# Scores of two tiles at once in every second step, a new order of the steps, and later first loads of values and words, in a chunked-attention, soft-MoE and SoLU kernel

## The chip, the cores and the metric

The kernel runs on one core of a Trainium2 chip. The metric is device time in microseconds (us), the median of several executions. Engines are called PE or TensorE (matrix products and transposes), DVE or VectorE, ACT or ScalarE, POOL or GpSimd, and SP, which issues the loads from HBM; the 16 DMA engines move the data.

## The reference, cut to what matters

```python
# attention inside chunks of 64 rows; q, k, v are (8, 8, 576, 64)
scores = scale * np.matmul(q_c, k_c.transpose(0, 1, 2, 4, 3))
scores = scores - np.max(scores, axis=-1, keepdims=True)
attn = np.exp(scores); attn = attn / (np.sum(attn, axis=-1, keepdims=True) + 1e-09)
x = np.matmul(attn, v_c)                     # then reshaped to (4608, 512)
# soft mixture of experts: 8 experts, 4 slots each
logits = x @ phi                             # (4608, 32)
d = softmax(logits, axis=0);  slot_input = d.T @ x
for e in range(E):
    h = np.maximum(slot_input[e] @ w1[e], 0.0);  slot_out[e] = h @ w2[e]
x = softmax(logits, axis=1) @ slot_out
# SoLU layer
h = x @ w_in;  solu = h * softmax(h)
ln = (solu - mean) / sqrt(var + 1e-06) * g_ln;  out = ln @ w_out
```

## The kernel before, in words

The 4608 rows are 36 tiles of 128. The first stage goes over the tiles in steps 0 to 33 (the last two tiles are in a list behind it). Each step works on several tiles at once, one behind the other: `S` makes the scores of tile i on PE (8 matmuls per tile), `mx` and `sub` take the row maximum and subtract it on DVE, `exp` is on ACT; `PT` transposes the result of tile i-1 and `PTe` copies it out of PSUM on ACT; `x` multiplies tile i-2 with the values, `rz`, `rc` and `xm` divide by the sums; `xT` transposes tile i-3, `xTe` copies it, and once in four steps `LT`, `L`, `mT`, `sl`, `z` and their helpers keep a running softmax over the rows. Beside it every step from 2 on converts one chunk c of the 64-bit words in which the SoLU weights are given: `t` (line 210) and `sq` (206) on ACT, `u` (213) and `a` (223) on DVE, `m` (219), `add` (229) and `mul` (233) on POOL. `m` needs the `sq` of its chunk, and the `sq` of the next chunk writes the buffer that `mul` reads, so one conversion follows the other in a ring over ACT and POOL.

The order of the operations of a step is written by hand: `STEP` has one line for each of the four kinds of steps (i modulo 4), and every engine gets its instructions in that order. Loads are issued by SP in the same order: `qk` loads the queries and keys of tile i+4 (two loads of 256 KB, into one of four buffers), `v` the values of two tiles, `raw` the words of two chunks, `W` the expert weights as far as the table `PACE` lets them. `FIRST` lists the loads ahead of step 0. The loads use eight semaphores in turn (DMAHW0 to DMAHW7), and a load waits until the load eight places before it has landed.

In the kernel before, the scores of even and odd tiles are the two halves of one PSUM tile `sx` (line 249). Behind the steps a list `ORDER` goes on: the last two tiles, the experts (lines 936, 973 and 987 multiply with `w1`, `w2` and the last columns of `w2`, as their weights come in), the combination with the slots, and from some 193 us on the SoLU output tiles, whose products are line 1393.

Of the kernel before, what the change touches and what calls it, by code (L numbers as in the profile page):

```python
# [9 lines left out]
F32 = mybir.dt.float32  # L10
# [7 lines left out]
PSUM = bass.MemoryType.PSUM  # L18
# [8 lines left out]


STEP = """
S a m t x xT u mT qk rz PT mx v xTe sub PTe W rc add mul raw exp xm mn d sq de  # L30
S a x u raw v m qk rz sl mx t W rc z xT sub xTe PT PTe add xm acc mul sq exp
m t S u a x qk rz xT mx W sub xTe PT rc acc v PTe add LT xm mul sq raw exp lte
t m a S x u raw L tm v mx xT add qk PT lall rz mul xTe sub rc PTe W sq xm exp
"""
PACE = [
    0, 0, 0, 0, 0, 0, 0, 1, 2, 2, 3, 4, 4, 5, 6, 6, 7, 8, 8, 9, 10, 10, 11, 12, 13, 13, 14, 15,
# [4 lines left out]
""".split()  # L41
AHEAD = 8
GATE = dict()
FIRST = "cs qk0 qk1 qk2 v0 raw0 qk3 g phi v2 raw2 raw4"
ORDER = """
cq1 cq2 cq3 cq4 cq5 cq6 cq7 S34 S35 loadw xT31 mx34 mx35 PT33 x32 xtev31 rz32 ptev33 sub34 LT31 lte7 ev32 own_c exp34
x33 own_q PT34 ptev34 xT32 L7 rz33 sub351 sub350 x34 exp350 PT350 exp351 ev33 xtev32 ptev0 xT33 PT351 lall7 LT32 rz34
# [20 lines left out]
def soft_moe_kernel(ctx: ExitStack, tc, qkT, v1, w12, w64, phi, g_ln, cst, out):  # L68
# [10 lines left out]
    cs = const.tile([128, 257], F32, name="cs")  # L79
# [18 lines left out]
    acc = mp.tile([128, 512], F32, name="acc")  # L98
# [136 lines left out]
    def cv_c(c):  # L235
# [1 line left out]

    first_loads = dict(
        qk0=lambda: load_qk(0), qk1=lambda: load_qk(1), qk2=lambda: load_qk(2), qk3=lambda: load_qk(3), v0=lambda: load_v(0), v2=lambda: load_v(2),
        **{f"raw{i}": lambda i=i: load_raw(i) for i in range(6)},  # L240
        cs=lambda: nc.sync.dma_start(out=cs, in_=cst), phi=lambda: nc.sync.dma_start(out=phi_sb, in_=phi),
        g=lambda: nc.sync.dma_start(out=g_sb, in_=g_ln),
    )
# [2 lines left out]

    p_t, pt_t, xps_t, x_t, lt_t, sps_t, mx_t = {}, {}, {}, {}, {}, {}, {}

    sx = ps1.tile([128, 2, 512], F32, name="s_ps")

    def pe_S(i):
        s = sx[:, i % 2, :]
        b = qk[i % 4]
        for g in range(4):
            for c in range(2):
                nc.tensor.matmul(  # L256
                    s[ts(c, 64), ts(g, 128)], b[:, 1, ts(2 * g + c, 64)], b[:, 0:3:2, ts(2 * g + c, 64)],
                    start=True, stop=True, tile_position=(0, 64 * c),
                )
        sps_t[i] = s.rearrange("p (h k) -> p h k", k=64)  # L260
# [210 lines left out]
    def step_ops(i):  # L471
        s0, s1, s2, s3, s4 = (blk(n, i) for n in (6, 7, 8, 9, 10))
        if i == NT - 3:
            s4 = s3
        c = cstep.get(i, NRAW)
        st = {}

        def rz():
            st["xp"] = x_view(xps_t[i - 2])
            st["rz"] = x_sums(st["xp"])  # L480

        def rc():
            mark("rc", nc.vector.reciprocal(out=st["rz"], in_=st["rz"]))

        def xm():
            x_t[i - 2] = x = XB[(i - 2) % 7]
            mark("xm", nc.vector.tensor_tensor(
                out=heads(x), in0=st["xp"][:, :, :, 0:64],
                in1=st["rz"].to_broadcast([128, 2, 4, 64]), op=ALU.mult,
            ))  # L490

        def W():
            load_w(pace[i + 1] - pace[i])

        cvc, x2, x3 = c < NRAW, i >= 2, i >= 3
        return dict(
            u=(cvc, lambda: cv_u(c)), m=(cvc, lambda: cv_m(c)), a=(cvc, lambda: cv_a(c)), add=(cvc, lambda: cv_s(c)),
            mul=(cvc, lambda: cv_w(c)), raw=(cvc, lambda: load_raw(c + 5)),
            sq=(True, lambda: cv_sq(cstep.get(i + 1, NRAW))), t=(True, lambda: cv_t(cstep.get(i + 1, NRAW))),
            S=(True, lambda: pe_S(i)), qk=(True, lambda: load_qk(i + 4)),  # L500
            mx=(True, lambda: soft_max(i)), sub=(True, lambda: soft_sub(i)), exp=(True, lambda: exp_S(i)),
            PT=(i >= 1, lambda: PTm(i - 1)), PTe=(i >= 1, lambda: PTe(i - 1)),
            x=(x2, lambda: pe_x(i - 2)), v=(i >= 1, lambda: load_v(i + 3)),
            rz=(x2, rz), rc=(x2, rc), xm=(x2, xm),
            xT=(x3, lambda: xTm(i - 3)), xTe=(x3, lambda: xTe(i - 3)), LT=(x3, lambda: pe_LT(i - 3)),
            lte=(s0 is not None, lambda: blk_a(s0)),
            L=(s1 is not None, lambda: pe_L(s1)), lall=(s1 is not None, lambda: blk_l(s1)),
            tm=(s1 is not None, lambda: run_max(s1)),
            mT=(s2 is not None, lambda: mTm(s2)), mn=(s2 is not None, lambda: mnv(s2)),
            d=(s2 is not None, lambda: dv(s2)),  # L510
            de=(s2 is not None, lambda: de(s2)),
            z=(s3 is not None, lambda: zm(s3)), sl=(s3 is not None, lambda: slm(s3)),
            acc=(s4 is not None, lambda: blk_e2(s4)), W=(True, W),
        )
# [63 lines left out]


    def x34():  # L580
        xps_t[n - 1] = x = sx
        pt = pt_t.pop(n - 1)
        for g in range(4):
            x_mm(n - 1, x, pt[:, g, :], g)
# [285 lines left out]

    def open_2():
        nonlocal e1, ps2, soT, cz, mx
        p1.close()
        e1 = pool("e1", 1)
        ps2 = pool("ps2", 1, p2, space=PSUM)
        T["hTb"] = e1.tile([128, 512], F32, name="hTb")
        soT = e1.tile([128, 4, 32], F32, name="soT")
        T["cP"] = e1.tile([128, 2, 128], F32, name="cP")
        cz = e1.tile([128, NT], F32, name="cz")
        mx = e1.tile([128, 9], F32, name="wmx")  # L880
# [617 lines left out]
```

## Time and profile before

| | us |
|---|---|
| three executions | 403.80, 402.84, 403.44 (median 403.44) |
| the profiled execution | 402.77 |
| its span in the trace | 401.0 |
| PE busy | 382.4 (95%) |
| DVE busy | 311.0 (78%) |
| ACT busy | 224.3 (56%) |
| POOL busy | 200.2 (50%) |

The span is the time from the first to the last instruction in the trace, and 1.77 us of the profiled execution lie outside it. The busy shares are means over all stages. The 16 DMA engines are busy all the time until about 181 us and only partly afterwards, so the first 181 us and the rest have to be read apart.

### The profile page before, as it was taken

What the parts mean: (1) busy time and instruction counts of PE and PEld (TensorE: products, weight loads), DVE (VectorE), ACT (ScalarE), POOL (GpSimd) and SP (SyncE); (2) the same over time, 40 slices, a digit from 0 to 9 for tenths busy, and PEclk for the clock granted to TensorE, in tenths of its full rate; (3) what the DMA queues carried; (4) which work ended last, traced back from release to release, by engine and by line L of the source; (5) the groups of instructions that cost most, each with busy time, mean ns of one, the idle gap of its engine ahead of it and who ended that gap; (6) DMA issues with size and microseconds to landing.
All of it is one profiled execution on the core that took longest, in us unless ns stands there. A gap on an engine that the chain in (4) does not pass through costs nothing. (4 is left out here: it accounts for less than half of the span.)

```text
span 401.0 us, 10317 instructions
## 1 busy us (share of the span) xinstructions
PE 382.4 (95%) x3947; PEld 220.4 (55%) x3947; DVE 311.0 (78%) x777; ACT 224.3 (56%) x470; POOL 200.2 (50%) x201
## 2 busy tenths in 40 slices
PE   3799899999999999999999999999999999999997
PEld 2577777777787642354544444444444444444445
DVE  3788788989886449574989799999888888888840
ACT  1577877877785512332577765556554555455521
POOL 2577767777778246330123255555455544454430
PEclk9999999999999999999999999999999999999999
DMA  7999999999999999991156757777665666557671
GB/s 231 403 409 408 389 397 397 409 407 407 410 397 408 401 396 406 409 391 26 30 103 146 140 134 159 159 158 148 144 140 135 144 151 133 132 137 158 132 159 52
DMA packets 101153, 99.20 MB, mean 247 GB/s; under 512 B 78064, under 2 KB 78704, under 8 KB 101104
## 3 DMA queue, kind: packets, MB, share of 16 engines
q1 hardware_dynamic: 101104, 98.54, 77.1%
q8 instruction: 31, 0.51, 0.5%
q14 instruction: 18, 0.15, 0.1%
HBM read 70.60 MB, written 9.44 MB: 200 GB/s over the span
## 5 line engine op out<-in xcount | busy, mean ns | idle before, releaser
L1194 POOL TENSOR_SCALAR uh<-u,sc 128x1024 f16<-128x1024 f32 (+1 forms) x35 | 65.1, 1860 | 51.1 <-issue 38.3
L1393 PEld LDWEIGHTS <-uhT 128*128 128x128 f16 x560 | 52.1, 98 | 68.3 <-issue 8.8
L1393 PE MATMUL o_ps<-xb,uhT 128*128 128x512 f16 x280 | 66.7, 380 | 0.7 <-DMA uhT<-uh 0.7
L1393 PE MATMUL o_ps<-xb,ulT 128*128 128x512 f16 x280 | 66.3, 379 | 0.0
L1393 PE MATMUL o_ps<-wo,uhT 128*128 128x512 f16 x280 | 66.1, 379 | 0.0
L1322 ACT ACTIVATE e<-h_ps,nm 128x1024 f32<-128x1024 f32 x34 | 37.8, 1113 | 43.7 <-DVE nm L1316 43.7
L1210 ACT ACTIVATE e<-u,nmean 128x1024 f32<-128x1024 f32 x35 | 40.1, 1147 | 28.7 <-DVE nmean L1209 28.7
L256 PE MATMUL s_ps<-qk 128*64 128x128 f32 x576 | 41.1, 287 | 9.3 <-DMA qk<-in_qkT 6.5
L1360 POOL TENSOR_TENSOR a<-a,mhalf 128x1 f32<-128x1 f32 x36 | 21.8, 606 | 56.2 <-DVE a L1377 42.5
L1316 DVE TENSOR_REDUCE nm<-h_ps 128x1 f32<-128x1024 f32 x34 | 41.5, 1220 | 9.3 <-PE h_ps L1311 9.3
L1185 DVE SCALAR_TENSOR_TENSOR u<-h_ps,e 128x1024 f32<-128x1024 f32 x35 | 42.8, 1223 | 6.1 <-ACT e L1322 6.1
L1393 PEld LDWEIGHTS <-ulT 128*128 128x128 f16 x280 | 27.3, 98 | 33.1 <-issue 0.3
L1370 DVE SCALAR_TENSOR_TENSOR ul<-u,sc,uh 128x1024 f16<-128x1024 f32 x35 | 45.3, 1295 | 0.0
L256 PEld LDWEIGHTS s_ps<-qk 128*64 128x64 f32 x576 | 32.5, 141 | 16.2 <-issue 10.3
L398 ACT ACTIVATE xt_b<-xt_ps 128x512 f32<-128x512 f32 (+1 forms) x37 | 21.6, 586 | 17.8 <-PE xt_ps L416 16.9
L265 DVE TENSOR_REDUCE mx<-s_ps 128x8 f32<-128x512 f32 x36 | 24.6, 684 | 8.5 <-PE s_ps L256 8.0
L1411 ACT ACTIVATE ob<-o_ps,a 128x512 f32<-128x512 f32 x35 | 23.8, 679 | 9.3 <-PE o_ps L1393 8.0
L219 POOL TENSOR_SCALAR conv<-conv 128x256 f32<-128x256 f32 x16 | 17.6, 1099 | 21.8 <-ACT conv L206 21.8
L1311 PE MATMUL h_ps<-s,c4T 128*128 128x512 f32 x68 | 27.4, 485 | 0.0
L277 ACT ACTIVATE p<-p 128x512 f32<-128x512 f32 x35 | 21.7, 621 | 6.6 <-DVE p L271 6.6
L271 DVE TENSOR_TENSOR p<-s_ps,mx 128x512 f32<-128x512 f32 x35 | 24.1, 690 | 0.9
L229 POOL TENSOR_TENSOR conv<-conv 128x256 int32<-128x256 int32 x32 | 23.3, 729 | 2.6
(232 smaller groups left out, 633.5 us busy)
## 6 DMA issues: line engine op xcount, KB each, us to landing
w<-in_w SPq DMA_DIRECT2D x45, 512.0 KB, 8.0
qk<-in_qkT SPq DMA_DIRECT2D x72, 256.0 KB, 6.8
vall<-in_v SPq DMA_DIRECT2D x18, 520.0 KB, 6.7
out<-ob SPq DMA_DIRECT2D x35, 256.0 KB, 2.1
raw<-in_w SPq DMA_DIRECT2D x16, 512.0 KB, 6.4
qk<-in_w SPq DMA_DIRECT2D x4, 512.0 KB, 9.0
w_raw<-in_w SPq DMA_DIRECT2D x3, 512.0 KB, 9.0
vall<-in_w SPq DMA_DIRECT2D x3, 512.0 KB, 8.9
```

Source lines behind the costliest of these rows:

```text
L256: nc.tensor.matmul(s[ts(c, 64), ts(g, 128)], b[:, 1, ts(2 * g + c, 64)], b[:, 0:3:2, ts(2 * g + c, 64)], start=True, stop=True, tile_posit ...
L265: mark("mx", nc.vector.tensor_reduce(out=mx, in_=s, axis=AX.X, op=ALU.max))
L271: mark("sub", nc.vector.tensor_tensor(out=p, in0=s, in1=mx.unsqueeze(2).to_broadcast([128, 8, 64]), op=ALU.subtract,))
L1185: nc.vector.scalar_tensor_tensor(out=u, in0=d["h"], scalar=1.0, in1=e, op0=ALU.mult, op1=ALU.mult, accum_out=zz[:, 1:2])
L1194: nc.gpsimd.tensor_scalar(out=uh[:, 0:n], in0=u[:, 0:n], scalar1=d["sc"][:, 1:2], scalar2=1.0, op0=ALU.mult, op1=ALU.mult)
L1210: nc.scalar.activation(out=d["e"], in_=d["u"], func=AF.Square, bias=nmean, scale=1.0, accum_out=d["zz"][:, 2:3])
L1311: nc.tensor.matmul(h[:, ts(n, 512)], c4T[:, i, :], s4[n], start=True, stop=True)
L1316: nc.vector.tensor_reduce(out=nm, in_=st[i]["h"], axis=AX.X, op=ALU.max, negate=True)
L1322: nc.scalar.activation(out=d["e"], in_=d["h"], func=AF.Exp, bias=d["nm"], scale=1.0, accum_out=d["zz"][:, 0:1])
L1370: nc.vector.scalar_tensor_tensor(out=ul, in0=d["u"], scalar=d["sc"][:, 1:2], in1=d["uh"], op0=ALU.mult, op1=ALU.subtract)
L1393: nc.tensor.matmul(d["o"], lt(n % 8), w(n % 8), start=(n == 0), stop=(n == 23))
L1411: nc.scalar.activation(out=ob, in_=d["o"], func=AF.Copy, scale=d["a"][:, 7:8])
```

## The change

The diff is short and stands here with one of the four lines of `STEP`. `pe_S` writes two separate PSUM tiles, `s0` and `s1`. In even steps it is called for tile i and tile i+1, one behind the other, and in odd steps not at all. The four lines of `STEP` are in a new order. In `FIRST` the loads `v2`, `raw2` and `raw4` are left out and `g` and `phi` go ahead of `qk3`; `v2` and `raw2` follow behind the q and k of tile 4 (step 0), `raw4` behind those of tile 5 (step 1). The two PSUM tiles are given back before the product of tile 34 and a tile of their old joint size takes their place.

```diff
--- before.py
+++ after.py
@@ -27,10 +27,10 @@
 
 
 STEP = """
-S a m t x xT u mT qk rz PT mx v xTe sub PTe W rc add mul raw exp xm mn d sq de
...
+S x t v m a rz xT u qk xTe PT mT PTe mx W sub add rc exp mul xm mn sq d raw de
...
 """
 PACE = [
     0, 0, 0, 0, 0, 0, 0, 1, 2, 2, 3, 4, 4, 5, 6, 6, 7, 8, 8, 9, 10, 10, 11, 12, 13, 13, 14, 15,
@@ -41,7 +41,8 @@
 """.split()
 AHEAD = 8
 GATE = dict()
-FIRST = "cs qk0 qk1 qk2 v0 raw0 qk3 g phi v2 raw2 raw4"
+FIRST = "cs qk0 qk1 qk2 v0 raw0 g phi qk3"
+THEN = {0: 'v2 raw2', 1: 'raw4'}
 ORDER = """
 cq1 cq2 cq3 cq4 cq5 cq6 cq7 S34 S35 loadw xT31 mx34 mx35 PT33 x32 xtev31 rz32 ptev33 sub34 LT31 lte7 ev32 own_c exp34
 x33 own_q PT34 ptev34 xT32 L7 rz33 sub351 sub350 x34 exp350 PT350 exp351 ev33 xtev32 ptev0 xT33 PT351 lall7 LT32 rz34
@@ -237,7 +238,7 @@
 
     first_loads = dict(
         qk0=lambda: load_qk(0), qk1=lambda: load_qk(1), qk2=lambda: load_qk(2), qk3=lambda: load_qk(3), v0=lambda: load_v(0), v2=lambda: load_v(2),
-        **{f"raw{i}": lambda i=i: load_raw(i) for i in range(6)},
+        **{f"raw{i}": lambda i=i: load_raw(i) for i in range(6)}, v4=lambda: load_v(4), v6=lambda: load_v(6),
         cs=lambda: nc.sync.dma_start(out=cs, in_=cst), phi=lambda: nc.sync.dma_start(out=phi_sb, in_=phi),
         g=lambda: nc.sync.dma_start(out=g_sb, in_=g_ln),
     )
@@ -246,10 +247,13 @@
 
     p_t, pt_t, xps_t, x_t, lt_t, sps_t, mx_t = {}, {}, {}, {}, {}, {}, {}
 
-    sx = ps1.tile([128, 2, 512], F32, name="s_ps")
+    pss = ctx.enter_context(ExitStack())
+    ps_s = pool("ps_s", 1, pss, space=PSUM)
+    s_banks = [ps_s.tile([128, 512], F32, name="s_ps", tag=f"s{a}") for a in range(2)]
+    sx = None
 
     def pe_S(i):
-        s = sx[:, i % 2, :]
+        s = s_banks[i % 2]
         b = qk[i % 4]
         for g in range(4):
             for c in range(2):
@@ -479,6 +483,11 @@
             st["xp"] = x_view(xps_t[i - 2])
             st["rz"] = x_sums(st["xp"])
 
+        def q():
+            load_qk(i + 4)
+            for o in THEN.get(i, "").split():
+                first_loads[o]()
+
         def rc():
             mark("rc", nc.vector.reciprocal(out=st["rz"], in_=st["rz"]))
 
@@ -497,7 +506,7 @@
             u=(cvc, lambda: cv_u(c)), m=(cvc, lambda: cv_m(c)), a=(cvc, lambda: cv_a(c)), add=(cvc, lambda: cv_s(c)),
             mul=(cvc, lambda: cv_w(c)), raw=(cvc, lambda: load_raw(c + 5)),
             sq=(True, lambda: cv_sq(cstep.get(i + 1, NRAW))), t=(True, lambda: cv_t(cstep.get(i + 1, NRAW))),
-            S=(True, lambda: pe_S(i)), qk=(True, lambda: load_qk(i + 4)),
+            S=(i % 2 == 0, lambda: (pe_S(i), pe_S(i + 1))), qk=(True, q),
             mx=(True, lambda: soft_max(i)), sub=(True, lambda: soft_sub(i)), exp=(True, lambda: exp_S(i)),
             PT=(i >= 1, lambda: PTm(i - 1)), PTe=(i >= 1, lambda: PTe(i - 1)),
             x=(x2, lambda: pe_x(i - 2)), v=(i >= 1, lambda: load_v(i + 3)),
@@ -578,6 +587,9 @@
 
 
     def x34():
+        nonlocal sx
+        pss.close()
+        sx = pool("ps_sx", 1, pss, space=PSUM).tile([128, 2, 512], F32, name="s_ps")
         xps_t[n - 1] = x = sx
         pt = pt_t.pop(n - 1)
         for g in range(4):
@@ -870,6 +882,7 @@
 
     def open_2():
         nonlocal e1, ps2, soT, cz, mx
+        pss.close()
         p1.close()
         e1 = pool("e1", 1)
         ps2 = pool("ps2", 1, p2, space=PSUM)
```

The first place is SP at the start, from the first words (`raw`, line 189 before and 190 after) on. Before, the words of chunks 2 to 5 are the last two rows but two:

```order
L189 DMA raw<-in_w 128x1024 [waits DMAHW0_49]
L176 DMA qk_114<-in_qkT 64x1024 [waits DMAHW1_49,DVE_49]
L176 DMA qk_114<-in_qkT 64x1024 [waits DMAHW2_49,Pool_49]
L242 DMA g_sb<-in_g_ln 128x8 [waits DMAHW3_49]
L241 DMA phi_sb<-in_phi 128x128 [waits DMAHW4_49]
L181 DMA vall<-in_v 128x1040 [waits DMAHW5_49]
L189 DMA raw<-in_w 128x1024 [waits DMAHW6_49]
L189 DMA raw<-in_w 128x1024 [waits DMAHW7_49]
L176 DMA qk_111<-in_qkT 64x1024 [waits DMAHW0_49,PE_49]
L176 DMA qk_111<-in_qkT 64x1024 [waits DMAHW1_49]
```

After, they are one by one behind the q and k of tiles 4 and 5 (buffers qk_111 and qk_112 for the second time):

```order
L190 DMA raw<-in_w 128x1024 [waits DMAHW0_49]
L243 DMA g_sb<-in_g_ln 128x8 [waits DMAHW1_49]
L242 DMA phi_sb<-in_phi 128x128 [waits DMAHW2_49]
L177 DMA qk_114<-in_qkT 64x1024 [waits DMAHW3_49,DVE_49]
L177 DMA qk_114<-in_qkT 64x1024 [waits DMAHW4_49,Pool_49]
L177 DMA qk_111<-in_qkT 64x1024 [waits DMAHW5_49,PE_49]
L177 DMA qk_111<-in_qkT 64x1024 [waits DMAHW6_49]
L182 DMA vall<-in_v 128x1040 [waits DMAHW7_49]
L190 DMA raw<-in_w 128x1024 [waits DMAHW0_49]
L177 DMA qk_112<-in_qkT 64x1024 [waits DMAHW1_49,PE_49]
L177 DMA qk_112<-in_qkT 64x1024 [waits DMAHW2_49]
L190 DMA raw<-in_w 128x1024 [waits DMAHW3_49]
```

The load of the second words (`raw`) moves from two places behind `phi` and the values to behind four halves of q and k; it now waits for DMAHW0, which is the first words' own semaphore, where before it waited for DMAHW6, a half of q and k.

The second place is PE in steps 8 and 9, in the middle of the first stage. Before:

```order
L256 MATMUL s_ps<-qk_111 64x128 [waits DMAHW4_49,DMAHW3_49,DVE_49]
L256 MATMUL s_ps<-qk_111 64x128 x7
L282 MATMUL x_ps<-vall,pt 64x65 [waits DMAHW0_49,DVE_49,Activation_49]
L282 MATMUL x_ps<-vall,pt 64x65 x15
L416 MATMUL xt_ps<-cs,xb_85 128x128 [waits PE_49]
L416 MATMUL xt_ps<-cs,xb_85 128x128 x3
L423 MATMUL mT_ps<-cs,ltb 128x128
L407 MATMUL pt_ps<-cs,p 128x128 [waits PE_49,Activation_49]
L407 MATMUL pt_ps<-cs,p 128x128 x3
L256 MATMUL s_ps<-qk_112 64x128 [waits DMAHW7_49,DMAHW0_49,DVE_49]
L256 MATMUL s_ps<-qk_112 64x128 x7
L282 MATMUL x_ps<-vall,pt 64x65 [waits DVE_49,Activation_49]
```

After:

```order
L260 MATMUL s_ps<-qk_111 64x128 [waits DMAHW4_49,DMAHW3_49]
L260 MATMUL s_ps<-qk_111 64x128 x7
L260 MATMUL s_ps<-qk_112 64x128 [waits DMAHW6_49,DMAHW5_49,DVE_49]
L260 MATMUL s_ps<-qk_112 64x128 x7
L286 MATMUL x_ps<-vall,pt 64x65 [waits DMAHW1_49,DVE_49,Activation_49]
L286 MATMUL x_ps<-vall,pt 64x65 x15
L420 MATMUL xt_ps<-cs,xb_85 128x128 [waits PE_49]
L420 MATMUL xt_ps<-cs,xb_85 128x128 x3
L411 MATMUL pt_ps<-cs,p 128x128 [waits Activation_49]
L411 MATMUL pt_ps<-cs,p 128x128 x3
L427 MATMUL mT_ps<-cs,ltb 128x128
```

The scores of step 9 have moved into step 8, ahead of that step's product with the values (`x_ps`), and the first of the two score groups has no wait for DVE any more; the second keeps one.

## Rows read from the trace of the kernel before

**Rows 1.** the page's first line
```profile
span 401.0 us, 10317 instructions
```

**Rows 2.** the chain of work that ended last: start us, us, what
```profile
206.86 5.35 PE o_ps L1393 x24
```

**Rows 3.** windows: busy us (instructions) per engine, then clock, DMA share, GB/s
```profile
15.00:20.00 5.00, 3.54 (x69) 2.85 (x70) 3.74 (x8) 2.96 (x7) 4.12 (x5) 1.00 1.03 414
40.00:45.00 5.00, 4.66 (x108) 3.74 (x108) 3.43 (x8) 4.33 (x11) 3.15 (x5) 1.00 0.99 385
45.00:50.00 5.00, 4.29 (x97) 3.81 (x98) 4.51 (x10) 3.67 (x12) 4.12 (x6) 1.00 1.01 392
55.00:60.00 5.00, 4.94 (x131) 3.98 (x125) 4.25 (x11) 3.92 (x11) 3.66 (x5) 1.00 1.03 389
60.00:65.00 5.00, 5.00 (x91) 4.25 (x88) 4.69 (x12) 4.21 (x11) 3.93 (x5) 1.00 1.01 384
65.00:115.00 50.00, 48.96 (x987) 38.19 (x990) 43.28 (x114) 37.84 (x102) 37.90 (x44) 1.00 1.03 408
115.00:120.00 5.00, 5.00 (x101) 4.29 (x90) 4.72 (x11) 3.99 (x12) 4.03 (x6) 1.00 1.00 385
```

**Rows 4.** what the load queue (SPq) waited for, 30 to 120 us
```profile
SPq L189 <- DVE conv L213: 19.4, 11, 2.5
SPq L181 <- PE L_ps L356: 7.2, 7, 1.9
```

**Rows 5.** TensorE in order of time: start, length (us), work, [idle before <-releaser]
```profile
72.01 1.09 PE L256 MATMUL s_ps<-qk 128*64 128x128 f32 x16
...
74.86 1.24 PE L256 MATMUL s_ps<-qk 128*64 128x128 f32 x16
...
85.88 1.09 PE L256 MATMUL s_ps<-qk 128*64 128x128 f32 x16
...
144.97 5.33 PE L936 MATMUL h_ps<-w,xl 128*4 128x512 f32 x48
...
182.63 1.08 PE L987 MATMUL h_ps<-w,hTb 128*4 128x128 f32 x32
```

**Rows 6.** the scores' line L256: what its matmuls sat idle for (us, times)
```profile
  DVE p L271: 5.3, 14
```

**Rows 7.** GpSimd in order of time, one conversion and the next
```profile
72.58 1.14 POOL L219 TENSOR_SCALAR conv<-conv,g_sb 128x256 f32<-128x256 f32 x1 [0.59 <-ACT conv L206]
...
76.00 1.25 POOL L219 TENSOR_SCALAR conv<-conv,g_sb 128x256 f32<-128x256 f32 x1 [0.66 <-ACT conv L206]
```

**Rows 8.** the first 20 us in order of time
```profile
7.90 0.69 DVE L271 TENSOR_TENSOR p<-s_ps,mx 128x512 f32<-128x512 f32 x1
...
8.69 1.98 PE L256 MATMUL s_ps<-qk 128*64 128x128 f32 x16 [1.56 <-DVE p L271]
...
9.77 1.53 SPq L189 DMA_DIRECT2D raw<-in_w  x2
...
12.55 0.45 ACT L210 ACTIVATE conv<-raw 128x256 int32<-128x256 uint32 x1 [3.30 <-DMA raw<-in_w]
...
12.59 1.12 SPq L176 DMA_DIRECT2D qk<-in_qkT  x2
...
17.57 0.42 ACT L210 ACTIVATE conv<-raw 128x256 int32<-128x256 uint32 x1
...
19.39 1.09 PE L256 MATMUL s_ps<-qk 128*64 128x128 f32 x16 [1.01 <-DMA qk<-in_qkT]
```

**Rows 9.** page, DMA issues: what, queue, count, KB each, median us to landing
```profile
raw<-in_w SPq DMA_DIRECT2D x16, 512.0 KB, 6.4
```

**Rows 10.** the weight loads L128 issued after 165 us, and issue to landing
```profile
L128 SPq DMA_DIRECT2D w<-in_w x6: 328/328/328, 165.5 to 171.9; - x6
...
DMA to landing us min/median/max: 10.2/10.4/10.4
```

More of the change, by code (lines that the diff above doesn't have):

```diff
@@ L29 @@
 STEP = """
-S a m t x xT u mT qk rz PT mx v xTe sub PTe W rc add mul raw exp xm mn d sq de
-S a x u raw v m qk rz sl mx t W rc z xT sub xTe PT PTe add xm acc mul sq exp
-m t S u a x qk rz xT mx W sub xTe PT rc acc v PTe add LT xm mul sq raw exp lte
-t m a S x u raw L tm v mx xT add qk PT lall rz mul xTe sub rc PTe W sq xm exp
+S x t v m a rz xT u qk xTe PT mT PTe mx W sub add rc exp mul xm mn sq d raw de
+S mx xT qk x PT a u sub z m W raw add PTe rz sl exp t rc mul xm v acc xTe sq
+S m mx t x u W a acc xT rz PT xTe raw add LT mul sub rc PTe v sq exp lte qk xm
+x u S qk a m v t add rz mx sub xT L raw PT tm PTe rc xTe mul xm lall sq exp W
 """
```

## The prediction

> **What bounds the kernel now.** I read the chain of waits first. It ends in one unbroken row of output products from 206.86 us on, 24 matmuls in 5.35 us and then the same again and again to the end of the span of 401.0 us [rows 1, 2]. Nothing of the change lies there, so the change can only move the moment at which that part begins. What decides the moment? The table of windows says it: from 10 us on the 16 DMA engines are full. Over 65 to 115 us their share is 1.03 and they move 408 GB/s, and only single stretches of 5 us fall below that, to 384 to 392 [rows 3]. PE is as full over the same 50 us (48.96). And the two end together. The last expert weight is issued at 171.9 us and lands 10.4 us later, at 182.3 [rows 10]; PE, which began with the experts at 144.97 and goes on with hardly a gap, starts the last 16 products at 182.63 and the half of them that needs the last weight some 0.5 us later [rows 5]. So the end of the kernel is the later of two things: the last byte of the load stream (182.3) and the end of PE's own sequence (183.7, from the start of stage one). A gain must move both; a loss needs only one.
>
> In the first stage the steps themselves run at 85.88 - 72.01 = 13.87 us for four steps [rows 5]. Three things ask for about that much. The loads fill the DMA engines at that pace. PE is full. And the conversion ring takes 3.42 us from one chunk to the next (72.58 to 76.00), of which POOL sits idle for 0.66 until ACT has squared the next chunk [rows 7]; that is 13.7 us for four.
>
> **The change part by part.** *Two score buffers, two tiles at once.* No work is added: 576 score matmuls stay 576. What goes is a wait. At the start the scores of tile 1 sat idle for 1.56 us until 8.69, until the subtraction of tile 0 (7.90 + 0.69) was over, though they write the other half of the tile [rows 8]. Over the whole stage these waits on `sub` are 5.3 us in 14 places [rows 6]. With separate tiles the first of a pair finds its buffer read long ago, and the second waits for a `sub` that belongs to the step before. I expect 3 to 5 of the 5.3 us to go from PE. But PE alone does not set the pace: the ring still needs 13.7 us and the loads about 13.8, so of 13.87 only 0.1 to 0.2 us per four steps is free, over seven such groups 0.5 to 1.5 us. The expert part of PE then starts that much earlier than 144.97; I take 1.0.
>
> The price of the pair is that `x`, `xT` and `PT` of an even step stand behind 2 x 1.09 us of scores in place of 1.09, and the `rz`, `xTe`, `PTe` that ACT does with them come 1.1 us later in that step; behind them on ACT stands `sq`, for which the ring waits. Odd steps give the 1.1 us back. The ring has 3.42 us per chunk with 0.66 of idle time; a late `sq` costs what it is late beyond that. Bounds: nothing, if POOL lags PE by that much anyway, and 1.1 us at each of 16 pairs. I take nothing, because the new order puts `sq` ahead of `exp` in two of the four lines, and because PE after the pair is ahead by the scores of the odd step.
>
> *The new order of the loads.* From 30 to 120 us SP stood for 19.4 us until the words' buffer was read by the conversion (`conv`, line 213) and for 7.2 us at the values, and every load behind stood with it [rows 4]. In the new lines `qk` of an odd step needs scores that were made a step before, and it and `W` stand ahead of `raw` and `v`; so the queue holds more when it stands. The five windows below 408 GB/s cost 5 x (23 + 16 + 19 + 24 + 23) / 408 = 1.29 us [rows 3]. This is all that can come back, unless the rate itself rises; nothing is the lower bound, because the share was 0.99 to 1.03 even there. I take 0.8, nearer to the upper end, since the same chip kept 408 for 50 us on end. The last weight then lands at 181.5.
>
> *The first loads.* No byte is added or left out. The second words now wait for the semaphore of the first words. These landed at about 12.55, when ACT's first `t` could run, and the load of q and k that waited for the same semaphore was issued at 12.59 [rows 8]. So `raw2` goes out at about 12.6 in place of 9.77, and with the median of 6.4 us [rows 9] it lands at 19.0. The third `t`, first of ACT's operations in step 3, ran at 17.57 [rows 8], so it may wait 1.4 us, and `PTe`, `xTe` and `sq` stand behind it. Against that the q and k of tile 4, for which PE waited until 19.39, are issued at about 9.3 to 10 in place of 12.59, and come some 3 us earlier. Bounds: a loss of 1.4 us and a gain of 3 for the steps, nothing for the stream, which is full either way. I take nothing; what the ring loses here it can regain in the steps behind, because POOL idles 0.66 of each turn.
>
> *The PSUM tile of tile 34.* It waited for the subtraction of tile 35 before and does so now. Nothing.
>
> **The sum.** Stream: 182.3 - 0.8. PE: 183.7 - 1.0, and it can't end before the last weight's products, which follow its landing by some 0.7 us in place of 1.4 (a last product group ends 1.08 us after its start, the last weight's half starts about 0.8 us behind the landing now and 0.3 then). So the part behind begins 1.0 us earlier by PE and up to 1.3 by the stream: 1.0. The profiled execution of 402.77 would become 401.8. It lies 0.67 below the median of 403.44, so the median becomes 402.4.
>
> The Trainium skill (DMA: Bandwidth & Descriptors, Where 436 GB/s comes from) puts the ceiling of the SBUF ports at 435 GB/s and says that for loads from HBM a limit near 358 binds. The trace disagrees with the second, 408 being held for 50 us, and no row here shows the first. By the one figure the stream could not be as fast as it is; by the other it would have 6% to give, which is a rival below.
>
> **The rivals.** *Nothing measurable.* The dips stay, because the DMA engines show a share of 0.99 to 1.03 even there and wait on something that is not SP; then the last weight lands at 182.3 as before and PE, though earlier, waits for it. Only the 0.3 to 0.5 us between landing and use is left: 403.0. For it speaks that the stream has no empty stretch; against it that the dips stand only where the steps are slower than later. Chance 0.28. That the two score buffers change nothing at all would end here too.
>
> *Slower: the ring.* `sq` comes late behind the longer even steps and the late `raw2`. If the stage ends more than about 0.5 us later, PE's row from 144.97 to 183.7 has no gap to take it up and the end moves with it. Half of the 1.1 us at a third of the 16 pairs is 2.9 us, of which the 1.0 taken above is given back: about +1.9, 405.3. From 0.4 us per pair on it decides the sign. Against it speaks the 0.66 us that POOL idles in each turn. Chance 0.20.
>
> *Much faster: the rate.* If better fed queues held 414 GB/s, the best of the windows [rows 3], over the 160 us from 20 to 180, in place of a mean of (25 x 387 + 135 x 408) / 160 = 404.7, the stream would end 160 x 9.3 / 414 = 3.6 us earlier, and if PE followed, 399.8. Against it: 50 us at 408 with full queues, and PE would need to be 3.6 us earlier too. Chance 0.04. The Trainium skill's 435 GB/s, from the same section, would give more than that; no run here shows it.
>
> **How the numbers follow.** The forecast, about 1.0 us faster, has 0.48, with 401.6 to 402.7 as its own range: the upper bound of both terms (1.3 from the dips and 0.5 between landing and use) at the low end, 0.7 at the other. A measurement of this kernel can tell about 0.2% or 0.8 us. Faster by more than that: 0.48 and 0.04. Within it: 0.28. Slower: 0.20. The range goes from 401.3, where all of the dips and the start are gained, to 404.6, which holds the lighter half of the slower case.
>
> **What would show it.** Right: scores in pairs with no wait on `sub` after the first steps; PE's first expert product near 144.0; the five windows near 408 GB/s; the last weight's landing near 181.5; the output products from 206.86 on as they were. Wrong: `t` at the start waiting for `raw` and the ring's turns longer than 3.42 us; a first expert product after 145.5; dips at the same or other places; or the experts' products waiting for weights while the landing has not moved.

## The result and the profile after

The changed kernel takes 406.74 us (median of 7 executions, 405.18 to 407.74), the kernel before 403.80 (7 executions, 402.84 to 404.20): 1.0072 times as long, 95% interval 1.0054 to 1.0090. It is slower by 2.9 us; 1.0 us faster was forecast. The profiled execution took 406.77 us, 4.0 more than that of before, and its span is 405.0, 4.0 more too.

TensorE in order of time, after. The first five rows answer to [rows 5] (tiles 20 and 24 are even, so they stand in pairs); the last is the second output tile.

```profile
68.81 1.97 PE L260 MATMUL s_ps<-qk 128*64 128x128 f32 x32
...
76.01 1.09 PE L260 MATMUL s_ps<-qk 128*64 128x128 f32 x16
...
90.41 1.97 PE L260 MATMUL s_ps<-qk 128*64 128x128 f32 x32
...
148.01 4.47 PE L949 MATMUL h_ps<-w,xl 128*4 128x512 f32 x40
...
185.67 1.08 PE L1000 MATMUL h_ps<-w,hTb 128*4 128x128 f32 x32
...
205.03 1.90 PE L1406 MATMUL o_ps<-xb,uhT 128*128 128x512 f16 x8 [1.56 <-DMA uhT<-uh]
```

Tile 8's scores begin at 32.59 us (before 32.74), so the start is level. The steps then lose: 14.40 us from tile 20 to tile 24, before 13.86. The first expert product comes 3.04 us later (148.01 against 144.97) and the last weight group 3.04 later (185.67 against 182.63): nothing between takes it up. The last 1.0 us is lost at the output tiles, where PE waits 1.56 us at the second one; before, the longest such wait was 0.67, at the third.

The table of windows, after, answering to [rows 3]:

```profile
40.00:45.00 5.00, 4.79 (x116) 4.06 (x120) 4.00 (x9) 4.14 (x12) 3.66 (x5) 1.00 1.02 403
45.00:50.00 5.00, 4.40 (x106) 3.84 (x101) 4.29 (x10) 3.43 (x10) 4.05 (x5) 1.00 1.03 408
55.00:60.00 5.00, 4.34 (x96) 3.58 (x92) 4.53 (x12) 2.80 (x8) 2.95 (x4) 1.00 1.01 402
60.00:65.00 5.00, 5.00 (x116) 4.37 (x111) 4.50 (x10) 3.70 (x11) 3.71 (x5) 1.00 0.94 343
65.00:70.00 5.00, 4.71 (x78) 3.41 (x78) 4.18 (x12) 4.39 (x12) 3.92 (x5) 1.00 0.96 348
65.00:115.00 50.00, 47.16 (x928) 37.21 (x927) 43.31 (x109) 37.00 (x98) 37.64 (x42) 1.00 1.02 403
115.00:120.00 5.00, 5.00 (x101) 4.09 (x101) 4.39 (x11) 3.60 (x10) 4.11 (x6) 1.00 1.01 400
```

Four of the five dips of before are filled, as foretold, but a new hole of 343 and 348 GB/s stands at 60 to 70 us. PE is busy 47.16 of the 50 us in which it was busy 48.96. What it waits for instead of the subtraction, matmuls only, 33 to 117 us:

```profile
PE x_ps L286 <- issue: 2.2, 4, 0.7
PE xt_ps L420 <- DVE xb L496: 1.7, 5, 0.6
PE s_ps L260 <- DVE conv L214: 0.4, 1, 0.4
PE xt_ps L420 <- issue: 0.4, 1, 0.4
PE pt_ps L411 <- issue: 0.2, 1, 0.2
```

"issue" says that nothing in the profile released the instruction: PE stood with its operands there. Before, no matmul of this stretch has such a wait of 0.2 us or more. Now there are six, 2.78 us, at 35.90, 43.27, 49.56, 57.43, 71.30 and 103.72 us, and one of 0.24 at 137.59: 3.02 us, where 3.04 are lost. The waits with a named releaser come to the same 2.1 us in this stretch, before and after. The scores wait for the subtraction in one place only, as expected. What the scores' line waited for, in place of [rows 6]:

```profile
  DMA qk<-in_qkT: 9.0, 8
  DVE p L275: 2.5, 1
```

This view, like that of [rows 6], counts weight loads and matmuls together, and the two overlap: from 33 to 117 us of the kernel before the weight loads are busy for 64.1 us and the matmuls for 81.5. Of the 9.0 us, 5.8 are the matmuls', before the very first scores; the other 3.2, in 7 places, are idle time of weight loads alone. The 5.3 us of [rows 6] fall apart in the same way (kernel before, 0 to 146 us):

```profile
PEld s_ps L256 <- DVE p L271: 3.1, 11, 0.6
PE s_ps L256 <- DVE p L271: 2.1, 3, 1.6
```

So the matmuls sat idle for the subtraction for 2.1 us, 1.56 of them at 8.69 us [rows 8]. What the load queue waited for from 30 to 120 us, in place of [rows 4]:

```profile
SPq L182 <- PE x_ps L286: 9.5, 8, 3.0
SPq L177 <- DMA w<-in_w: 5.8, 7, 0.9
SPq L190 <- DVE conv L214: 5.5, 5, 1.4
```

SP's stand at the words' buffer fell from 19.4 to 5.5 us, but in all SP stood for 40.7 us, before 37.9. The stand went elsewhere: to the values' buffer, which the values' products free (14.2, before 10.5), to q and k (14.3, before 5.0) and to the weights (5.4, before 2.2).

### The profile page after: what moved, and what is told of

The parts are those of the page before. It is cut to its first block, busy times and chain, and to the rows that moved or that the text cites. A ratio compares the mean times of both kernels' runs of the same rounds, so it can differ in the third digit from the quotient of the medians.

```text
span 405.0 us, 10332 instructions
## 1 busy us (share of the span) xinstructions
PE 381.7 (94%) x3947; PEld 221.4 (55%) x3947; DVE 313.4 (77%) x777; ACT 224.0 (55%) x470; POOL 200.0 (49%) x201
## 4 chain that ended last, share of the span: by engine, by line
PE 74%; issue 8%; DVE 6%; POOL 5%; ACT 3%; DMA 3%; SPq 1%; DVEq 0%; ACTq 0%; POOLq 0%
PE o_ps L1406 44%; PE s_ps L260 5%; PE x_ps L286 4%; PE h_ps L1324 4%; PE xt_ps L420 3%; PE h_ps L949 3%; PE pt_ps L411 2%; PE h_ps L986 2%; POOL conv L220 2%; DMA raw<-in_w 2%; POOL xb L1092 1%; DVE xb L496 1%; PE o_ps L1416 1%; PE sl_ps L471 1%; DMA uhT<-uh 1%
## 5 line engine op out<-in xcount | busy, mean ns | idle before, releaser
L1207 POOL TENSOR_SCALAR uh<-u,sc 128x1024 f16<-128x1024 f32 (+1 forms) x35 | 64.0, 1830 | 51.2 <-issue 38.3
L1335 ACT ACTIVATE e<-h_ps,nm 128x1024 f32<-128x1024 f32 x34 | 37.9, 1114 | 44.7 <-DVE nm L1329 43.9
L260 PE MATMUL s_ps<-qk 128*64 128x128 f32 x576 | 37.5, 284 | 8.7 <-DMA qk<-in_qkT 5.8
L220 POOL TENSOR_SCALAR conv<-conv 128x256 f32<-128x256 f32 x16 | 17.7, 1104 | 23.6 <-ACT conv L207 23.6
L286 PE MATMUL x_ps<-vall,pt 64*64 64x65 f32 x1088 | 25.2, 225 | 3.4 <-issue 2.2
L402 ACT ACTIVATE pt<-pt_ps 128x512 f32<-128x512 f32 x35 | 20.9, 597 | 13.1 <-PE pt_ps L411 13.1
L420 PE MATMUL xt_ps<-cs,xb 128*128 128x128 f32 x140 | 22.8, 284 | 3.8 <-DVE xb L496 2.3
```

What stands on the lines that cost most here:

```text
L260: nc.tensor.matmul(s[ts(c, 64), ts(g, 128)], b[:, 1, ts(2 * g + c, 64)], b[:, 0:3:2, ts(2 * g + c, 64)], start=True, stop=True, tile_posit ...
L286: nc.tensor.matmul(x[ts(c, 64), a, ts(g, 65)], pt[ts(a, 64), ts(c, 64)], vall[ts(a, 64), i % 6, ts(2 * g + c, 65)], start=True, stop=True, ...
L402: A=lambda o, i: nc.scalar.activation(out=o, in_=i, func=AF.Copy),
L420: nc.tensor.transpose(t[:, g, :], x_t[i][:, ts(g, 128)], ident)
L1207: nc.gpsimd.tensor_scalar(out=uh[:, 0:n], in0=u[:, 0:n], scalar1=d["sc"][:, 1:2], scalar2=1.0, op0=ALU.mult, op1=ALU.mult)
L1335: nc.scalar.activation(out=d["e"], in_=d["h"], func=AF.Exp, bias=d["nm"], scale=1.0, accum_out=d["zz"][:, 0:1])
```

## The experiments

### Which part costs it

At first there were three theories: the pair costs it (P), the new order of the lines (O), or the first loads (F). Four kernels, each the kernel before with part of the change. The first has the two buffers alone (the old lines, the old first loads):

```diff
-    sx = ps1.tile([128, 2, 512], F32, name="s_ps")
+    s_banks = [ps_s.tile([128, 512], F32, name="s_ps", tag=f"s{a}") for a in range(2)]
```

> The kernel before with the two score buffers alone: scores of one tile in each step, old order of the lines, old first loads. Theory P (the pair costs the time: two tiles' scores ahead of the values' products, and q and k of the odd tile used one step earlier): nothing is lost here; the waits on the subtraction (5.3 us in 14 places) go from PE, and the time is 402.8 to 403.8, -0.2% to 0. Theory O (the new order of the four lines costs it): the same, as the lines are old. Theory F (the first loads cost it): the same. My prediction's own term for PE would make it up to 1.0 us faster, 402.8. All would fall if this alone were slower by 1 us or more.

Measured: 406.54 us, ratio 1.0058 (1.0038 to 1.0077). No theory foretold it, and by what was said ahead of it all three fall. The first expert product is at 147.93, as late as in the changed kernel.

The second has the first loads alone:

```diff
-FIRST = "cs qk0 qk1 qk2 v0 raw0 qk3 g phi v2 raw2 raw4"
+FIRST = "cs qk0 qk1 qk2 v0 raw0 g phi qk3"
+THEN = {0: 'v2 raw2', 1: 'raw4'}
```

> The kernel before with the new first loads alone: the second values and words behind q and k of the first steps. Theory F: slower, 405 to 407, most of the 3 us. Theories P and O: within 0.8 us of the kernel before, since tile 8's scores start at 32.59 us in the changed kernel against 32.74 before; the loss there is built after that.

Measured: 403.88 us, ratio 1.0001 (0.9989 to 1.0013). F falls; the prediction's "nothing" for the first loads was right.

The third has buffers and pairs in the old order:

```diff
-            S=(True, lambda: pe_S(i)),
+            S=(i % 2 == 0, lambda: (pe_S(i), pe_S(i + 1))),
```

> The kernel before with two buffers and the scores of two tiles in every second step, the lines otherwise in the old order, old first loads. Theory P: slower, 405 to 408, since the pair is all that matters, and scores wait for q and k as in the changed kernel. Theory O: within 0.8 us of the kernel before, 403 to 404.6, since the old lines keep the conversion's square and the other places.

Measured: 409.82 us, ratio 1.0147 (1.0125 to 1.0168), 3.3 us above the buffers alone. The waits show where the pair has its price: in an odd step no scores stand any more between a transposition and the values' products that need it back from ACT.

```profile
PEld x_ps L286 <- ACT pt L402: 6.2, 7, 1.0
...
PE x_ps L286 <- ACT pt L402: 4.6, 6, 0.8
```

The changed kernel has 0.4 us of these: its new lines put `xT` in between.

The fourth has the new lines and two buffers, but single scores (against the changed kernel; its first loads are the old ones too):

```diff
-            S=(i % 2 == 0, lambda: (pe_S(i), pe_S(i + 1))),
+            S=(True, lambda: pe_S(i)),
```

> The changed kernel's new lines and two buffers, but the scores of one tile in each step (at the place where the letter S stands in each line), old first loads. Theory O: slower, 405 to 407. Theory P: within 0.8 us of the kernel before, 402.6 to 404.2, with the first expert product near 145 us in place of 148.0 and no wait of scores for q and k after 33 us.

Measured: 412.83 us, ratio 1.0222 (1.0196 to 1.0248). So the parts don't add up: the new order costs 6.3 us more than the old one without the pair, and saves 3.1 with it. Neither P nor O explains why two buffers alone, which add no work and take waits away, cost 2.6 us. In that kernel's trace this stands at the place where most is lost at once:

```profile
102.65 0.56 PE L286 MATMUL x_ps<-vall,pt 64*64 64x65 f32 x20
103.98 0.45 PE L286 MATMUL x_ps<-vall,pt 64*64 64x65 f32 x12 [0.76 <-issue]
```

PE stops in the middle of 32 equal matmuls, all released together, with no weights or operands to wait for. What can be late there is the code. The page of every kernel has a DMA queue for it (before):

```profile
q8 instruction: 31, 0.51, 0.5%
q14 instruction: 18, 0.15, 0.1%
```

31 packets of 16 KB on q8 fit PE alone: 3947 matmuls and 3947 weight loads are 7894 instructions, 30.8 packets of 256; with the 155 semaphore and drain records of PE's sequencer they are 8049, 31.4 packets. In the view of DMA queues, in windows of 0.1 us, one such packet moves at 55.35 us and PE goes on at 57.91; one at 101.45, and PE goes on at 103.98. From here on the theory is C: PE waits for its own code.

### Moving the code

Tiny matmuls ahead of the first scores, where PE waits some 5 us for q and k in any case, shift all later code within its packets and change nothing else (16 of them are 64 instructions):

```diff
+    for _ in range(16):
+        nc.tensor.matmul(s_banks[0][0:1, 0:1], mhalf, mhalf, start=True, stop=True)
```

> The kernel before with 16 one-by-one matmuls added ahead of the first scores, where PE waits some 5 us for q and k anyway: 64 instructions more, so that every later instruction of PE stands 64 places further in its code, which is loaded in packets of 16 KB. Theory C (PE waits for its own code where a packet comes late behind the load stream): stalls without a releaser can appear, at new places; the kernel before had none between 13 and 130 us, so only a loss is possible: 403.5 to 406.5. Theory Q (the odd tile's q and k come late; code plays no part): no change, 403.2 to 404.6.

Measured: 404.57 us, ratio 1.0015 (0.9999 to 1.0031), single executions from 403.54 to 406.06. The profiled one, 406.06, has its first expert product at 147.98, 3.0 later than before, and stalls of 1.31, 0.79 and 0.43 us that the kernel before has not. The median lies within what either theory foretold, so the time decides nothing; the stalls at new places speak for C.

> The changed kernel with the same 64 instructions ahead. Theory C: the stalls without a releaser (2.8 us between 33 and 104 us, in five products of the values and transposes) move to other instructions, about a quarter of the 6.6 us between packets earlier in the program; the time may change by 1 us or more to either side. Theory Q: the same places, the same 405.9 to 407.5.

Measured: 405.00 us, ratio 1.0028 (1.0013 to 1.0043): 64 instructions that do nothing make the changed kernel 1.7 us faster. Two stalls are left, 1.10 us, and the first expert product is at 146.37.

> The changed kernel with 32 such matmuls, 128 instructions, half a packet. Theory C: stalls at places half a packet earlier in the program, a time that may differ by 1 us or more from that of the changed kernel. Theory Q: 405.9 to 407.5 and stalls where they were.

Measured: 406.55 us, ratio 1.0068 (1.0043 to 1.0093); stalls of 1.85 and 0.76 us.

All these stalls lie where the packets end. Count PE's records in the trace in order of time: matmuls, weight loads, and the semaphore and drain records of its sequencer (an fp32 product has four, two passes of a weight load and a matmul; a transposition has two). Ahead of each of the 52 stalls of 0.2 us or more between 20 and 140 us, in eighteen of the twenty kernels, those further below too, the count divided by 256 leaves 193, 194 or 195. Places without a rule would leave anything from 0 to 255. And ahead of each of them a q8 packet had moved 2.2 to 2.8 us before PE went on.

The order of the two tells more. Take every place where the count leaves 193 as a packet's end. From some 15 to 140 us, in all kernels but one, exactly one q8 packet moves between one end and the next, and PE never passes an end less than 2.2 us behind that packet. In the kernel before the packet moves 3.6 us behind the last end on average, in the changed kernel 4.1, and the ends lie 6.6 and 6.8 us apart. So the next end comes 3.0 and 2.7 us behind the packet on average, not much above that 2.2.

By this count the profile puts some stalls at packet ends down to others. Here is one of the kernel before, and below it one of the changed kernel, whose packets had moved 2.3 and 2.4 us ahead of them:

```profile
49.18 0.60 PE L416 MATMUL xt_ps<-cs,xb 128*128 128x128 f32 x4 [0.49 <-PE x_ps L282]
...
77.56 1.09 PE L260 MATMUL s_ps<-qk 128*64 128x128 f32 x16 [0.45 <-DVE conv L214]
```

With them, code stalls of 0.2 us or more behind 33 us are 3.5 us in the changed kernel and 0.7 in the kernel before: 2.7 of the 3.04 us. In the kernel with the two buffers alone they are 2.1 us, 1.3 more than before, and its first expert product is 2.96 late, so there the rest is not explained by code.

Here are the 0.69 us of the changed kernel in TensorE's order of time,

```profile
102.44 0.58 PE L286 MATMUL x_ps<-vall,pt 64*64 64x65 f32 x24
103.72 0.34 PE L286 MATMUL x_ps<-vall,pt 64*64 64x65 f32 x8 [0.69 <-issue]
```

and its DMA queue for code in the window 101.3 to 101.4 us (packets, MB, share of 16 engines):

```profile
q8 instruction: 1, 0.02, 68.2%
```

In the kernel shifted by 64 the stall stands in the products of tile 17, where the changed kernel stalls in those of tiles 10, 12, 16 and 25 (the packet: within 71.6 to 71.8 us):

```profile
72.85 0.65 PE L288 MATMUL x_ps<-vall,pt 64*64 64x65 f32 x26
74.18 0.34 PE L288 MATMUL x_ps<-vall,pt 64*64 64x65 f32 x6 [0.68 <-issue]
```

The Trainium skill (Runtime: NRT & Kernel Launch, Instruction fetch mechanics) says that the sequencer fetches code in blocks of 16 KiB, 256 instructions, while it works on the block before, and calls the cost mostly hidden. The blocks agree with the 31 packets and the 256 above, and the time agrees with the one packet between two ends; the cost is hidden in the kernel before but for 0.7 us, and in the changed kernel it is 3.5 us.

### What makes a packet late

The loads in halves, here that of the words, and likewise the values and weights:

```diff
-nc.sync.dma_start(out=raw.rearrange("p k n t -> p (k n t)"), in_=w64[c // 2].bitcast(U32))
+for h in range(2):
+    nc.sync.dma_start(out=raw[ts(h, 64)].rearrange("p k n t -> p (k n t)"), in_=w64[c // 2].bitcast(U32)[ts(h, 64)])
```

> The changed kernel with every load of expert weights, values and words as two loads of half the partitions. As no more than eight loads are out at once, fewer bytes stand ahead of anything that is asked for. Theory C: a code packet follows the boundary sooner (mean 3.7 us or less in place of 4.4), stalls fall from 2.8 us to under 1, and the stage ends 1 to 3 us earlier, unless the stream itself gets slower: 403.5 to 405.5. Theory Q: q and k too land earlier (5 us or less in place of 7), so the 3.2 us of waits for them go; the stalls without a releaser stay at 2 to 3 us. Neither: 406 to 408, because more loads are issued.

Measured: 523.00 us, ratio 1.2945 (1.2908 to 1.2982). Two loads over half the partitions each move 238 GB/s where one over all moved 387 in the same stretch of the changed kernel, so this tells nothing of the code:

```profile
60.00:90.00 30.00, 22.18 (x312) 17.83 (x316) 14.23 (x33) 10.72 (x29) 12.30 (x15) 0.73 1.01 238
```

The Trainium skill (SBUF — State Buffer, Can I just issue two DMAs to hit both halves?) says so: two transfers to two halves do not add up, and only one that spans all 128 partitions reaches all ports. The trace agrees as to the rate.

Then the stage without the expert weights' stream; the weights are loaded behind it, so only the stage is read.

```diff
-PACE = [
-    0, 0, 0, 0, 0, 0, 0, 1, 2, 2, 3, 4, 4, 5, 6, 6, 7, 8, 8, 9, 10, 10, 11, 12, 13, 13, 14, 15,
-    16, 16, 17, 18, 19, 22, 25, 25,
-]
+PACE = [0] * 36
```

> The kernel before without the loads of expert weights inside the steps (the table that paces them is all zeros; they all come behind the steps, so the total time grows and says nothing). What is read is the stage: the start of the scores of tiles 8 and 34. Both theories: the stage runs at PE's or the ring's own pace; 90.6 us from tile 8 to tile 34 now, at most 90 here.

> The changed kernel without those loads, read as the run beside it. Theory C (PE waits for its code, which comes late behind a full load stream): with the stream half empty the stalls without a releaser vanish (2.8 us between 33 and 104 us to under 0.3) and tiles 8 to 34 take no longer than in the kernel before without those loads (+0.5 us or less, against +3.2 with them). Theory O (the pair or the new order itself is slower on the engines): the stage stays 2 to 3 us longer than that of the kernel before.

In all they took 427.16 and 424.40 us. Measured, the changed kernel: no stall without a releaser, tiles 8 to 34 in 90.15 us, and

```profile
32.58 1.97 PE L257 MATMUL s_ps<-qk 128*64 128x128 f32 x32
...
122.73 1.97 PE L257 MATMUL s_ps<-qk 128*64 128x128 f32 x32
...
143.89 5.33 PE L946 MATMUL h_ps<-w,xl 128*4 128x512 f32 x48
```

143.89 is 1.08 us earlier than in the kernel before with its stream, and theory O is dead: by engines alone the new stage is no slower. The kernel before without the stream took 92.79 us for those tiles, above the 90 expected, mostly because it now has stalls of 0.49 and 1.87 us, at 255 to 304 GB/s; without them it would be 90.43. Its first expert product is at 147.23. So a packet can be late without a full stream, though the stream has a part in it: without the weights a packet moves 2.9 us behind the last end on average, in place of 3.6, and in the changed kernel 2.6 in place of 4.1. And being on time is no lasting virtue of the kernel before.

Small loads between the large ones, to have fewer bytes queued:

```diff
     def gated(what, r):
+        nc.sync.dma_start(out=ticks[nt[0] % 16][0:1], in_=g_ln[0:1])
+        nt[0] += 1
```

> The kernel before with a load of 32 bytes ahead of each load of words, values and expert weights. As eight loads are out at most, these take up places and fewer bytes are queued (about 2.0 MB in place of 3.1). Theory C: the code packets come sooner; the kernel before had no stall, so its time stays or falls by the 0.5 us that single executions lose: 403 to 404.5, unless the stream loses its rate, then slower.

> The changed kernel with the same small loads. Theory C with the queue as the reason for the lateness: loads land after some 5 us in place of 7, stalls without a releaser under 1 us, waits for q and k under 1 us; 404 to 405.5. Theory O or a lateness that has nothing to do with the queue: 406 or more, with stalls as before. If the stream is starved by so short a queue, the stage is slower at 400 GB/s or less and this tells nothing.

Measured: 426.04 and 424.32 us, ratios 1.0534 (1.0497 to 1.0571) and 1.0496 (1.0465 to 1.0527). The stream is starved (360 and 352 GB/s at 60 to 90 us), so the times say little. But the loads of words landed after 6.1 us in place of 7.2 in the changed kernel and it stalled for 4.1 us, the other for none: less in the queue was not enough to bring the packets in time.

### Late q and k

Both tiles' loads go into the even step, and `qk` in the third line moves from the end to behind `u`:

```diff
-            load_qk(i + 4)
+            if i % 2 == 0:
+                load_qk(i + 4)
+                load_qk(i + 5)
```

> The changed kernel with q and k of two tiles loaded in the even step, ahead of weights, words and values there, so that the odd tile's come a step sooner. If the late q and k of the odd tile cost time beside the code (3.2 us of waits between 33 and 117 us), these waits fall below 1 us and the time to 404.5 to 405.9. If they only sit where another wait would stand, the waits go and the time stays within 0.8 us of the changed kernel. The code packets may shift with the changed times: stalls anywhere from 0 to 3 us.

Measured: 407.20 us, ratio 1.0089 (1.0057 to 1.0120). The waits for q and k did not fall; between 33 and 117 us they are 5.1 us in place of 3.0. These are idle times of the weight loads; the matmuls waited for q and k for 0.2 us there. The run without weights had 5.4 us of them and lost nothing.

> The same with the 64 instructions ahead, which gave the changed kernel 405.0. If code stalls and q and k add up, 403.5 to 404.5; if q and k don't matter, 404.5 to 405.5.

> The same with 192 instructions ahead: a new place of the packets, stalls that can't be foretold; first expert product at 145.0 plus the sum of the stalls behind 33 us, within 0.8 us, if nothing but the code makes the stage longer. The time follows: 403.2 plus that sum.

> The changed kernel with 192 instructions ahead and q and k as in it. First expert product at 145.3 plus the sum of the stalls behind 33 us, within 0.8 us (145.3 is what the run shifted by 64 had without its 1.1 us).

Measured: 407.95 us (407.51 without one execution of 411.86), 407.40 and 407.87 us, ratios 1.0117 (1.0078 to 1.0157), 1.0090 (1.0065 to 1.0115) and 1.0104 (1.0062 to 1.0145). All missed. The second had stalls of 1.85 us and its first expert product at 148.32, 1.5 above what was foretold from them; the third had 2.9 us behind 33 us and 147.32, 0.9 below. So with the stream on, a stall isn't always paid in full, and other waits move too. The other executions of the first range from 405.73 (the profiled one) to 409.12.

### Code without work, work without code

```diff
         s = sx[:, i % 2, :]
+        for _ in range(8):
+            nc.tensor.matmul(s[0:1, 0:1], mhalf, mhalf, start=True, stop=True)
```

> The kernel before with eight one-by-one matmuls ahead of each tile's scores: 32 instructions more per step, so a 16 KB packet of PE's code lasts five steps' worth less: 256 instructions in place of 6.6 us of steps are used up in some 5.5. Theory C: from one packet's boundary to the use of the next take about 3.7 us until it moves and 2.5 us behind that, 6.2 us, longer than a packet lasts; nearly every packet then stalls PE, stalls without a releaser sum up to 6 to 15 us between 33 and 117 us, and the time is 410 to 425, at least 5 us above the run with one wide matmul in their place. Against theory C: hardly any stall, and the time within 3 us of that run.

The control has one `nc.tensor.matmul(s[0:1, 0:160], mhalf, cs[:, 0:160], ...)` there instead.

> The control to the run beside it: the kernel before with one matmul of 160 columns ahead of each tile's scores, 4 instructions and about as much time on PE (some 0.3 us) as the eight small ones. PE is full, so the 36 of them cost about 0.3 us each: 408 to 414, with few stalls without a releaser (under 2 us between 33 and 117 us).

Measured: 421.02 us (1.0424, 1.0363 to 1.0485) with more code and 411.01 (1.0193, 1.0149 to 1.0238) with the wide matmul. The 10 us between them look like theory C, but the stalls refuse: 1.4 us between 33 and 117 us in place of 6 to 15. The small matmuls simply take long themselves, some 0.47 us per step by the distance to the scores behind them:

```profile
86.57 0.54 PE L254 MATMUL s_ps<-mhalf 128*1 128x1 f32 x16
87.04 1.09 PE L258 MATMUL s_ps<-qk 128*64 128x128 f32 x16
```

0.47 in 36 steps is 17 us, near the 15.5 by which the first expert product is late. Between 23.6 and 129.2 us the code packets came every 5.9 us there, nearly all in time. A fixed round trip of 6.2 us, which I had worked out from boundaries and packets of the kernel before, does not exist. That stalls fall on packet boundaries is shown; why a single packet is late stays open.

## Why the prediction was wrong, point by point

- *What bounds the kernel.* Right in its form: PE's row to the end of the experts has no gap, and 3.04 us lost in the stage arrive at the end in full. Wrong in that nothing of the change could touch the part behind: 1.0 us more is lost at the output tiles. A packet of PE's code moved at 202.35 us, 2.7 before PE went on at 205.03, which looks like a late packet, but the count there leaves 213, so no packet ends at it; and the kernels shifted by 64 and 128 wait 1.27 and 1.40 us at the third tile without a packet near. PE waited for a DMA transpose (`uhT`) that was issued 3.05 us later than in the kernel before (200.31, before 197.26) and took 4.7 us to land, before 3.1. Why it took longer is open.
- *The waits on the subtraction.* Right in that they went: one place, 2.5 us at the start, is left of 14. Wrong in what they were worth. The prediction took the 5.3 us as idle time of PE over the whole stage; 3.1 of them are weight loads', and of the matmuls' 2.1 only 0.6 lie behind the start.
- *PE: -1.0.* This is the step that failed, in two ways. It expected 3 to 5 of the 5.3 us back for PE, of which 0.6 us were there to be had behind the start. And it set free PE's time against the ring and the loads alone, and took PE's own code to be always there. In the changed kernel the code stalls without a releaser are 3.02 us (3.5 with the one at 77.56), in the kernel before 0.26 (0.7 with the one at 49.18). The stage's first expert product moved by +3.04; less the 3.02 it would stand at 144.99, and in the kernels shifted by 64 and 128, less their stalls, at 145.27 and 145.48, so with the stream on also the gain of 1.0 is missing (the kernel before less its 0.26 stands at 144.71). Without the weights' stream it stands at 143.89, where 144.0 was forecast, but that number is in part luck. The kernel before without that stream and less its stalls stands at 144.87, 0.98 later; of this the stage from tile 8 to 34 makes 0.3 us, and 0.7 lie ahead of tile 8, which began at 33.29 us there and at 32.74 in the kernel before with the stream.
- *The pair's price: nothing.* Right for the pair and its new order together, since without the stream tiles 8 to 34 take 90.15 us, against 90.43 in the kernel before less its stalls (one execution each); wrong for the pair alone, which costs 3.3 us in the old lines, not through a late `sq` but through values' products that wait for ACT's copy.
- *The stream: -0.8.* Four of five dips were filled, though SP stood no less in all (40.7 us, before 37.9), but 60 to 70 us lost (65 + 60) x 5 / 408 = 1.5 us, more than the 1.29 that could come back. The last weight is issued at 173.3 and lands 10.2 us later, at 183.5; that PE's stalls keep the buffers and so the loads back is likely, but only argued.
- *The first loads, the PSUM tile of tile 34.* Nothing, as said; the first was measured alone.
- *The rival "slower: the ring".* Its sign, its test (a first expert product after 145.5) and the missing gap came true, not its mechanism: POOL's waits for `sq` grew from 17.0 to 18.3 us over 33 to 117, 0.05 per turn.

No version of these beats the kernel before: the nearest, its order with the new first loads, is the same within 0.13%.

## What to carry to other kernels

When an engine that is full stops in the middle of a run of equal instructions with no releaser, count its records, those of its sequencer too, and look for a code packet a few us earlier: many small matmuls use up 256 instructions in 6.6 us here, and the stalls move when a handful of idle instructions is put ahead. Before idle time is taken as an engine's, see whether the view counts its weight loads too. Before a small gain or loss is put down to an order of work, run the same kernel with its code shifted; here that alone moved the time by 1.7 us, more than the gain that was forecast. And test the parts of a change in all the combinations that run: pair and order each cost several us alone, and little together.

## What the hardware showed that I had not expected

- Late code on TensorE: 52 stalls of 0.2 to 2.3 us, all 193 to 195 records behind a multiple of 256, each ending 2.2 to 2.8 us behind the packet, in executions with 245 to 406 GB/s of loads (33 to 117 us).
- In nineteen of the twenty kernels a packet of code moved only when PE was past the end of the one before: 3.6 us past it on average in the kernel before, 4.1 in the changed one.
- One 32-byte load ahead of each large one took the stream of the kernel before from 404 to 360 GB/s, and halving the loads by partitions took that of the changed kernel from 387 to 238 (60 to 90 us).
- Kernels with the same work and order, 64 to 192 idle instructions apart, have medians from 405.0 to 407.9 us, and single executions of one of them (shifted by 192) lie 5.2 us apart.
